# Widening float64 weights on VectorE and ScalarE alone, squaring in PSUM, and a new order of the first third

## The chip, the cores and the metric

The kernel runs on one core of one Trainium2 chip. Its metric is the device time of one execution in microseconds (us); 1429.37 us is the median of three executions before the change (1426.54 to 1430.47). The engines are named as the profile names them: PE is TensorE (PEld its weight loads), DVE is VectorE, ACT is ScalarE, POOL is GpSimd, and SP issues the DMAs. Each engine runs its own instructions in a fixed order and waits on semaphores for the others.

## What is computed

A linear attention with an exponential feature map, then a dense two-layer network with squared ReLU, then a mixture of four experts over all tokens:

```python
proj = x @ w_phi                                   # x is q or k: 4 batches, 8 heads, 576 tokens, 64 wide
proj = proj - max(abs(proj))                       # over the 128 features
phi  = concat(exp(proj), exp(-proj))
kv, z = phi(k).T @ v, sum(phi(k))
attn = (phi(q) @ kv) / (phi(q) @ z + 1e-6)         # 2304 tokens, 512 wide
h = relu(attn @ w_in)                              # 512 x 2048
x = (h * h) @ w_out                                # 2048 x 512
p = domain_probs / sum(domain_probs)
out = sum_e p[:, e] * (relu(x @ w1[e]) @ w2[e])    # 4 experts, 512 x 1024 x 512
```

`w_in` and `w_out` arrive as float64, and the kernel reads each number as two 32-bit words.

## The kernel before

Every product is made of three single-precision products: an operand is split into a rounded high part and the remainder, its low part, and low*high, high*low and high*high are summed in PSUM. A split is a copy (the method `copy`, line 78 on ACT, line 80 on DVE) and a subtraction (`sub`, line 83, on DVE or POOL).

The work has three stages. **The front** takes the first third of the time. In it 16 pairs of heads (`Pair`, four batches of four pairs) go through attention: transposes, a projection, `shift` (absolute maximum and subtraction, lines 231 and 239, on DVE), exponentials on ACT, and small matmuls. Beside them the first two batches go through the dense network: eight groups `fg` of two chunks of 128 hidden units, each chunk with two matrices (`Matrix`, one from `w_in`, one from `w_out`, so 32 in all, each 128 x 512), and for each group and batch a `Unit`: `hidden` (line 516), `relu`, `square`, `g_hi`, `g_lo` for two chunks, then four `out` (line 563) and `add` (line 571). Each of the 32 matrices is loaded, widened from float64 to single precision (lines 457 to 477), stored to DRAM for later use, and split (`hi` on ACT, `lo` on POOL). **The second stage** runs the dense network for the other two batches with a seven-product scheme (`PairUnit`), and **the third** the experts. Both are built from times in a plan (`plan_tail`) and follow on an unchanged code path.

All steps of the front, and the first of the second stage, stand in one table: `PLACES` gives each step of each object its place in one sequence (1788 places before), and the steps are issued in that sequence, so the table sets the order on every engine and on SP's DMA queue. The tile pools decide what waits for what: `ps_m` has three PSUM banks of 128 x 512 and holds the hidden products `ph`, the outputs `pm`, and in the first nine pairs the attention's small products; `ps_a` has three banks, `ps_p` one larger tile. A bank is given to the next product when its last reader is done.

In `widen`, four DVE instructions build the number's bits: `top` (line 457, a shift and a mask; line 460, the sign), `one` (line 464, the power of two), and `wf` (line 465, the low word times that power). POOL adds `top` to `wf` (line 470), ACT squares the high word (line 474) and DVE multiplies `wf` by a comparison with that square (line 477), which sets tiny numbers to zero. In `Unit`, ACT writes relu(ph) to an SBUF tile `r`, DVE overwrites `r` with max(ph, 0)*r (line 539), ACT copies it to `gh`, and POOL subtracts to get `gl`.

Of the kernel before, what the change touches and what calls it, by code (L numbers as in the profile page):

```python
# [8 lines left out]
F32 = mybir.dt.float32  # L9
# [12 lines left out]
def fused_kernel(  # L22
# [68 lines left out]
    make_identity(nc, ident)  # L91
    wd = const.tile([P, 2 * NF], F32, name="wd")
# [339 lines left out]
    class Matrix:  # L432
# [17 lines left out]
        def widen(self):  # L450
            self.f = pools["w"].tile([P] + self.shape, F32, tag=self.tag + "f", name="wf", bufs=WB[self.tag])
            self.dst = dst = self.f if len(self.shape) == 1 else self.f.rearrange("p k f -> p (k f)")
            low, high = self.raw[:, :, 0], self.raw[:, :, 1]
            self.top = top = cpool.tile([P, DM], U32, tag="top", name="top", bufs=1)
            self.one = one = cpool.tile([P, DM], U32, tag="one", name="one", bufs=2)
# [8 lines left out]
            nc.vector.tensor_scalar(out=one, in0=top, scalar1=0xFF800000, scalar2=None, op0=ALU.bitwise_and)  # L464
            nc.vector.scalar_tensor_tensor(  # L465
                out=dst, in0=low, scalar=2.0**-52, in1=f32(one), op0=ALU.mult, op1=ALU.mult
            )
# [4 lines left out]
        def widen_mask(self):  # L472

            nc.scalar.activation(out=f32(self.one), in_=f32(self.raw[:, :, 1]), func=AF.Square)

        def widen_flush(self):
            nc.vector.scalar_tensor_tensor(
                out=self.dst, in0=f32(self.one), scalar=(2.0**-15 * 1.125) ** 2, in1=self.dst,
                op0=ALU.is_ge, op1=ALU.mult,
            )  # L480
# [41 lines left out]
    class Unit:  # L522
# [14 lines left out]
        def square(self, i):  # L537
            r = self.r[i]
            nc.vector.scalar_tensor_tensor(
                out=r, in0=self.p.pop(i)[:, : self.n], scalar=0.0, in1=r, op0=ALU.max, op1=ALU.mult  # L540
            )
# [31 lines left out]
    def new_x2(b):  # L573
# [797 lines left out]
```

## Time and profile before

| | |
|---|---|
| median of three executions | 1429.37 us (1426.54 to 1430.47) |
| the profiled execution | 1428.52 us, of which the profile's span is 1426.7 us |
| granted TensorE clock, mean over the span | 0.989 |
| busy share of the span | PE 96%, DVE 69%, ACT 41%, POOL 54% |
| chain of work that ended last, by engine | PE 78%, DVE 13%, issue 3%, POOL 3%, ACT 2% |
| DMA | 97.41 MB, mean 68 GB/s |

Busy time is the union of an engine's instructions. PE's matmuls overlap, so a busy PE may still not be at its peak. An instruction of DVE or POOL that waits for access to memory counts as busy, so one that takes far longer than the shortest of its kind has waited. The chain is followed back from the last instruction, at each step to whatever released it.

### The profile page before, as it was taken

To read this page: it belongs to the slowest core of one execution; us is meant where nothing else is said; L and a number is where in the kernel's file an instruction comes from. 1 tells how busy PE (TensorE), PEld (TensorE's weight loads), DVE (VectorE), ACT (ScalarE), POOL (GpSimd) and SP (SyncE) were. 2 spreads that over 40 slices of the span, in tenths; PEclk is the share of its full clock that TensorE was granted. 3 is DMA by queue.
4 is the path that set the end of the run, shared out by engine and by line. 5 is a ranking of instruction groups with operands and counts; after the bars stand their busy time and mean duration, and the time that the engine had idled before them with its cause. 6 is when DMAs were issued, how large, how long until landed. Compare 5 with 4: busy or idle time off the path is not lost.

```text
span 1426.7 us, 18682 instructions
## 1 busy us (share of the span) xinstructions
PE 1371.4 (96%) x6906; PEld 1142.2 (80%) x6906; DVE 977.9 (69%) x1305; ACT 579.0 (41%) x1034; POOL 764.4 (54%) x541
## 2 busy tenths in 40 slices
PE   8899998999988999999999999999999999999998
PEld 6677787877765888887788888887788888888887
DVE  6888899999978465667655565558655555555554
ACT  5677786666644533424232223224231221322321
POOL 2666867676859675677544444444544343442430
PEclk9999999999999999999999999999999999999999
DMA  6343423444253111101111121111311020110102
GB/s 149 91 101 91 130 83 104 127 132 120 85 149 108 36 60 31 44 15 60 60 59 55 35 60 60 53 37 37 111 60 30 30 60 30 45 45 30 45 1 74
DMA packets 136938, 97.41 MB, mean 68 GB/s; under 512 B 70288, under 2 KB 113424, under 8 KB 136848
## 3 DMA queue, kind: packets, MB, share of 16 engines
q1 hardware_dynamic: 136848, 96.23, 23.0%
q8 instruction: 55, 0.90, 0.3%
q14 instruction: 35, 0.29, 0.1%
HBM read 80.32 MB, written 15.80 MB: 67 GB/s over the span
## 4 chain that ended last, share of the span: by engine, by line
PE 78%; DVE 13%; issue 3%; POOL 3%; ACT 2%; DVEq 0%; POOLq 0%; ACTq 0%
PE pa L1205 27%; PE pz L1130 7%; PE pv L1130 7%; PE px L1130 7%; PE pa L1183 7%; PE pa L1160 5%; PE py L1130 4%; PE pm L563 2%; PE ph L516 2%; DVE top L460 2%; PE pm L326 2%; DVE one L464 1%; PE pm L360 1%; DVE top L457 1%; DVE mx L231 1%
## 5 line engine op out<-in xcount | busy, mean ns | idle before, releaser
L83 POOL TENSOR_TENSOR w<-f,w 128x1024 fp32r<-128x1024 f32 (+1 forms) x80 | 184.9, 2329 | 277.7 <-ACT w L78 277.7
L1214 DVE SCALAR_TENSOR_TENSOR x<-pa,prob,x 128x512 f32<-128x512 f32 x270 | 201.8, 750 | 131.6 <-PE pa L1205 131.6
L1205 PE MATMUL pa<-w2l,gh 128*128 128x512 f32 x576 | 225.0, 391 | 3.5 <-DVE x L1214 2.8
L1205 PE MATMUL pa<-w2h,gl 128*128 128x512 f32 x576 | 224.8, 390 | 1.0 <-DVE gl L1108 1.0
L1205 PE MATMUL pa<-w2h,gh 128*128 128x512 f32 x576 | 224.8, 390 | 0.0
L1137 ACT ACTIVATE u<-px 128x512 f32<-128x512 f32 x40 | 23.9, 597 | 454.2 <-PE px L1130 452.8
L83 POOL TENSOR_TENSOR w2l<-f,w2h 128x1024 fp32r<-128x1024 f32 x40 | 96.0, 2400 | 141.3 <-ACT w2h L78 141.3
L1102 ACT ACTIVATE gh<-u 128x512 fp32r<-128x512 f32 x136 | 85.9, 631 | 166.3 <-DVE u L1140 151.5
L1205 PEld LDWEIGHTS pa<-w2l,gh 128*128 128x128 f32 x576 | 108.4, 188 | 26.3 <-DVE x L1214 3.2
L1205 PEld LDWEIGHTS pa<-w2h,gl 128*128 128x128 f32 x576 | 108.4, 188 | 24.4 <-DVE gl L1108 1.8
L1033 POOL TENSOR_TENSOR f<-f 128x256 f32<-128x256 f32 x160 | 125.2, 803 | 3.3
L1205 PEld LDWEIGHTS pa<-w2h,gh 128*128 128x128 f32 x576 | 108.5, 188 | 21.9
L83 POOL TENSOR_TENSOR q<-qf,q 128x128 fp32r<-128x128 f32 (+1 forms) x64 | 100.0, 1578 | 46.5 <-DVE q L80 42.6
L1130 PE MATMUL pv<-oh,w 128*128 128x512 f32 x320 | 98.6, 389 | 1.8 <-POOL w L83 1.8
L1130 PE MATMUL px<-oh,w 128*128 128x512 f32 x320 | 99.5, 392 | 0.0
L1130 PE MATMUL pz<-oh,w 128*128 128x512 f32 x320 | 98.7, 390 | 0.0
L1140 DVE TENSOR_TENSOR u<-pz,u 128x512 f32<-128x512 f32 x80 | 55.3, 691 | 51.3 <-PE pz L1130 50.3
L1108 DVE SCALAR_TENSOR_TENSOR gl<-u,gh 128x512 fp32r<-128x512 f32 x96 | 72.3, 762 | 24.9 <-ACT gh L1102 23.5
L78 ACT ACTIVATE w<-f 128x1024 fp32r<-128x1024 f32 (+1 forms) x80 | 77.0, 1009 | 10.8 <-POOL f L1033 10.8
L1140 DVE TENSOR_TENSOR u<-py,u 128x512 f32<-128x512 f32 x40 | 27.6, 690 | 76.0 <-PE py L1130 42.9
L470 POOL TENSOR_TENSOR wf<-wf,top 128x512 f32<-128x512 f32 x32 | 46.2, 1445 | 57.6 <-DVE wf L465 48.0
L1160 PEld LDWEIGHTS pa<-rest,w 128*128 128x128 f32 x576 | 73.7, 195 | 1.9
(150 smaller groups left out, 3332.3 us busy)
## 6 DMA issues: line engine op xcount, KB each, us to landing
f<-in_moe_w_dram SPq DMA_DIRECT2D x96, 256.0 KB
raw<-in_moe_w_in_dram SPq DMA_DIRECT2D x16, 512.0 KB
raw<-in_moe_w_out_dram SPq DMA_DIRECT2D x16, 512.0 KB
f<-in_moe_w_dram SPq DMA_DIRECT2D x64, 128.0 KB
rec<-one SPq DMA_DIRECT2D x32, 144.0 KB
qk<-in_q_dram SPq DMA_DIRECT2D x32, 128.0 KB
qk<-in_k_dram SPq DMA_DIRECT2D x32, 128.0 KB
va<-in_v_dram SPq DMA_DIRECT2D x32, 128.0 KB
```

The lines of the kernel that those rows point to most:

```text
L78: nc.scalar.activation(out=dst, in_=src, func=AF.Copy)
L83: eng.tensor_tensor(out=dst, in0=a, in1=b, op=ALU.subtract)
L470: nc.gpsimd.tensor_tensor(out=self.dst, in0=self.dst, in1=f32(self.top), op=ALU.add)
L1033: nc.gpsimd.tensor_tensor(out=s[:, i], in0=a, in1=b, op=op)
L1102: nc.scalar.activation(out=self.gh, in_=self.r, func=AF.Copy if self.square else AF.Relu)
L1108: nc.vector.scalar_tensor_tensor(out=self.gl, in0=self.src, scalar=0.0, in1=f32(self.gh), op0=ALU.max, op1=ALU.subtract)
L1130: nc.tensor.matmul(p, lhsT=a, rhs=m, start=start and i == 0, stop=i == len(ops) - 1, skip_group_check=not start)
L1140: nc.vector.tensor_tensor(out=self.u[out], in0=self.p[a], in1=self.u[b], op=ALU.add)
L1160: nc.tensor.matmul(q, lhsT=a[:, s, k], rhs=m[:, kk], start=kk + j == 0, stop=kk == KD - 1 and j == 2)
L1183: nc.tensor.matmul(self.p[:, :n], lhsT=a, rhs=m, start=i == 0, stop=i == len(ops) - 1)
L1205: nc.tensor.matmul(self.p, lhsT=a, rhs=m, start=i == 0, stop=i == len(ops) - 1)
L1214: nc.vector.scalar_tensor_tensor(out=o, in0=p, scalar=pe, in1=o, op0=ALU.mult, op1=ALU.add)
```

## The change

The 32 widenings no longer use POOL. Two DVE masks take the exponent bits (`power`) and the fraction bits (`wf`) out of the high word; ACT turns the exponent bits into those of a single-precision power of two, and the fraction bits into 1 + fraction; DVE adds the low word, puts the sign on the power, and multiplies. Per matrix that is five DVE instructions and two on ACT, where five on DVE, one on ACT and one on POOL stood. In `Unit` the square stays in the PSUM bank of the hidden product, ACT and DVE read it there, and the low half is a DVE subtraction in place of a POOL one. `PLACES` is a new table throughout, now of 1852 places. A one-column constant is added.

```diff
+    exponent = const.tile([P, 1], F32, name="exponent")
+    nc.gpsimd.memset(exponent, -8.0 * 0x38000000)
...
         def widen(self):
...
-            nc.vector.tensor_scalar(
-                out=top, in0=high, scalar1=3, scalar2=0x3FFFFFFF, op0=ALU.logical_shift_left, op1=ALU.bitwise_and
+            self.power = cpool.tile([P, DM], U32, tag="power", name="power", bufs=2)
+            for out_, mask in ((self.power, 0x7FF00000), (self.dst.bitcast(U32), 0x000FFFFF)):
+                nc.vector.tensor_scalar(out=out_, in0=high, scalar1=mask, scalar2=None, op0=ALU.bitwise_and)
+
+        def widen_power(self):
+            nc.scalar.activation(out=self.power, in_=self.power, func=AF.Relu, scale=8.0, bias=exponent)
+
+        def widen_one(self):
+            nc.scalar.activation(out=self.dst, in_=self.dst.bitcast(U32), func=AF.Copy, scale=2.0**-20, bias=1.0)
+
+        def widen_add(self):
+            nc.vector.scalar_tensor_tensor(
+                out=self.dst, in0=self.raw[:, :, 0], scalar=2.0**-52, in1=self.dst, op0=ALU.mult, op1=ALU.add
             )
+
+        def widen_sign(self):
             nc.vector.scalar_tensor_tensor(
-                out=top, in0=high, scalar=0xC0000000, in1=top, op0=ALU.bitwise_and, op1=ALU.bitwise_or
+                out=self.power, in0=self.raw[:, :, 1], scalar=0x80000000, in1=self.power,
+                op0=ALU.bitwise_and, op1=ALU.bitwise_or,
             )
...
-        def widen_add(self):
-            nc.gpsimd.tensor_tensor(out=self.dst, in0=self.dst, in1=f32(self.top), op=ALU.add)
...
+        def widen_mul(self):
+            nc.vector.tensor_tensor(out=self.dst, in0=self.dst, in1=f32(self.power), op=ALU.mult)
...
         def square(self, i):
...
+            p, r = self.p[i][:, : self.n], self.r.pop(i)
+            nc.vector.scalar_tensor_tensor(out=p, in0=p, scalar=0.0, in1=r, op0=ALU.max, op1=ALU.mult)
 
         def g_hi(self, i):
             gh = pools["g"].tile([P, 512], F32R, tag="gh", name="gh")
-            copy(nc.scalar, gh[:, : self.n], self.r[i])
+            copy(nc.scalar, gh[:, : self.n], self.p[i][:, : self.n])
 
         def g_lo(self, i):
             gl = pools["g"].tile([P, 512], F32R, tag="gl", name="gl")
-            sub(nc.gpsimd, gl[:, : self.n], self.r.pop(i), f32(self.g[i][0][:, : self.n]))
+            sub(nc.vector, gl[:, : self.n], self.p.pop(i)[:, : self.n], f32(self.g[i][0][:, : self.n]))
...
     PLACES = {
         ("", "load_wd"): (
-            1,
+            7,
         ),
...
```

DVE near the end of the front, where the last matrices are widened; `raw` holds the float64 words of one matrix, `wf` its widened form, `ph` a hidden product, `x2` an output sum. Before:

```order
L457 TENSOR_SCALAR top_4953<-raw_4862 128x512
L460 SCALAR_TENSOR_TENSOR top_4953<-raw_4862,top_4953 128x512
L464 TENSOR_SCALAR one_4954<-top_4953 128x512
L465 SCALAR_TENSOR_TENSOR wf_4952<-raw_4862,one_4954 128x512
L477 SCALAR_TENSOR_TENSOR wf_4889<-one_4891,wf_4889 128x512
L457 TENSOR_SCALAR top_4994<-raw_4983 128x512
L460 SCALAR_TENSOR_TENSOR top_4994<-raw_4983,top_4994 128x512
L464 TENSOR_SCALAR one_4995<-top_4994 128x512
L465 SCALAR_TENSOR_TENSOR wf_4993<-raw_4983,one_4995 128x512
L477 SCALAR_TENSOR_TENSOR wf_4952<-one_4954,wf_4952 128x512
```

After:

```order
L458 TENSOR_SCALAR power_4951<-raw_4922 128x512
L458 TENSOR_SCALAR wf_4950<-raw_4922 128x512
L481 TENSOR_TENSOR wf_4737<-wf_4737,power_4738 128x512
L541 SCALAR_TENSOR_TENSOR ph_4866<-ph_4866,r_4928 128x512
L571 TENSOR_TENSOR x2_1_104<-pm_4930,x2_1_104 128x512
L475 SCALAR_TENSOR_TENSOR power_4951<-raw_4922,power_4951 128x512
L470 SCALAR_TENSOR_TENSOR wf_4950<-raw_4922,wf_4950 128x512
L83 TENSOR_TENSOR gl_5001<-ph_4866,gh_4978 128x512
L481 TENSOR_TENSOR wf_4950<-wf_4950,power_4951 128x512
```

The block of four widening instructions in a row is broken into a pair, a pair and a single one, with reads of PSUM between them, and `gl` has come to DVE.

POOL in the second half of the front; `q` are the low parts of the query features (`2x512` is the large form), `wl` those of a weight matrix, `va` those of v. Before:

```order
L83 TENSOR_TENSOR gl_4337<-r_4145,gh_4326 128x512
L173 MEMSET va_4353 128x9x2
L83 TENSOR_TENSOR gl_4371<-r_4150,gh_4279 128x512
L83 TENSOR_TENSOR wl_4409<-wf_4300,wh_4389 128x512
L83 TENSOR_TENSOR q_4450<-qf_4238,q_4298 128x2x512
L83 TENSOR_TENSOR q_4450<-qf_4245,q_4298 128x2x64
L83 TENSOR_TENSOR q_4461<-qf_4245,q_4453 128x2x64
L470 TENSOR_TENSOR wf_4443<-wf_4443,top_4444 128x512
L470 TENSOR_TENSOR wf_4518<-wf_4518,top_4519 128x512
L83 TENSOR_TENSOR gl_4562<-r_4369,gh_4545 128x512
```

After:

```order
L83 TENSOR_TENSOR wl_4563<-wf_4363,wh_4487 128x512
L83 TENSOR_TENSOR q_4561<-qf_4434,q_4417 128x2x512
L83 TENSOR_TENSOR va_4724<-va_4403,va_4594 128x594
L83 TENSOR_TENSOR wl_4749<-wf_4429,wh_4648 128x512
L83 TENSOR_TENSOR q_4771<-qf_4632,q_4745 128x2x64
L83 TENSOR_TENSOR q_4773<-qf_4632,q_4747 128x2x64
L83 TENSOR_TENSOR wl_4796<-wf_4583,wh_4794 128x512
L83 TENSOR_TENSOR q_4771<-qf_4742,q_4745 128x2x512
```

The additions to `wf` and the `gl` subtractions are gone from POOL; `q`, `wl`, `va` and the division stay.

SP's queue at the start; `wd` is the feature projection's weight, `raw` a float64 matrix. Before:

```order
L145 DMA qk<-in_q_dram 128x4x64
L145 DMA qk<-in_k_dram 128x4x64
L98 DMA wd<-in_w_phi_dram 64x128
L99 DMA wd<-in_w_phi_dram 64x128
L444 DMA raw<-in_moe_w_in_dram 128x4x256
```

After:

```order
L446 DMA raw<-in_moe_w_out_dram 128x1024
L147 DMA qk<-in_q_dram 128x4x64
L147 DMA qk<-in_k_dram 128x4x64
L145 DMA qk<-in_q_dram 128x1x64
L145 DMA qk<-in_k_dram 128x1x64
L147 DMA va<-in_v_dram 128x4x64
L147 DMA qk<-in_q_dram 128x4x64
L147 DMA qk<-in_k_dram 128x4x64
L100 DMA wd<-in_w_phi_dram 64x128
L101 DMA wd<-in_w_phi_dram 64x128
```

A weight matrix is now loaded first, and `wd` has moved from the third and fourth place to the ninth and tenth. On PE the twenty warming transposes of the identity (line 191), which stood first, now stand behind five transposes of queries and keys.

## Rows read from the trace of the kernel before

**Rows 1.** Stretches: busy us of PE, PEld, DVE, ACT, POOL; clock; DMA.

```profile
200.00:300.00 100.00, 91.34 (x522) 76.12 (x521) 96.91 (x117) 67.53 (x139) 70.18 (x50) 0.98 0.40 112
...
490.00:600.00 110.00, 109.93 (x578) 94.51 (x577) 59.71 (x91) 40.98 (x64) 70.68 (x53) 1.00 0.14 44
600.00:1400.00 800.00, 793.24 (x3719) 664.26 (x3718) 477.98 (x651) 225.52 (x313) 365.85 (x254) 1.00 0.15 45
```

**Rows 2.** The same view, the front as one stretch.

```profile
0.00:440.00 440.00, 403.15 (x2316) 330.56 (x2317) 390.72 (x513) 286.82 (x619) 286.85 (x214) 0.98 0.41 114
```

**Rows 3.** Chain that ended last: the span by engine, 0 to 440 by line.

```profile
PE 78%; DVE 13%; issue 3%; POOL 3%; ACT 2%; DVEq 0%; POOLq 0%; ACTq 0%
...
by line: issue 9.6%; PE pm L563 7.7%; PE ph L516 7.3%; DVE top L460 7.1%; PE pm L326 6.7%; DVE one L464 3.9%; PE pm L360 3.9%; DVE top L457 3.7%; DVE mx L231 3.3%; PE pa L326 2.9%; DVE kf L83 2.8%; PE pp L223 2.7%; DVE x L571 2.4%; PE pp L2
```

**Rows 4.** DVE groups, 0 to 440: count, busy us, mean ns, idle before.

```profile
L460 DVE SCALAR_TENSOR_TENSOR top<-raw,top 128x512 uint32<-128x512 uint32 x32 | 47.9, 1497 | 1.1
...
L477 DVE SCALAR_TENSOR_TENSOR wf<-one,wf 128x512 f32<-128x512 f32 x32 | 38.0, 1190 | 1.1 <-POOL wf L470 0.8 <-ACT one L474 0.3
L571 DVE TENSOR_TENSOR x<-pm,x 128x512 f32<-128x512 f32 x49 | 32.7, 680 | 8.9 <-PE pm L563 8.6
L465 DVE SCALAR_TENSOR_TENSOR wf<-raw,one 128x512 f32<-128x512 uint32 x32 | 31.6, 988 | 1.7
L457 DVE TENSOR_SCALAR top<-raw 128x512 uint32<-128x512 uint32 x32 | 30.1, 941 | 1.8 <-POOL wf L470 1.8
L464 DVE TENSOR_SCALAR one<-top 128x512 uint32<-128x512 uint32 x32 | 25.4, 793 | 1.1
...
L83 DVE TENSOR_TENSOR tl<-pa,th 128x512 fp32r<-128x512 f32 x32 | 21.7, 679 | 5.6 <-ACT th L78 5.5
```

**Rows 5.** Those widening lines one by one: shortest, median, longest in ns.

```profile
L457 DVE TENSOR_SCALAR top<-raw x32: 409/788/2553, 12.4 to 426.9; 128x512 uint32<-128x512 uint32 x32
L460 DVE SCALAR_TENSOR_TENSOR top<-raw,top x32: 691/1655/2772, 12.9 to 427.8; 128x512 uint32<-128x512 uint32 x32
L464 DVE TENSOR_SCALAR one<-top x32: 426/428/2500, 13.6 to 429.5; 128x512 uint32<-128x512 uint32 x32
L465 DVE SCALAR_TENSOR_TENSOR wf<-raw,one x32: 691/693/1809, 14.1 to 430.1; 128x512 f32<-128x512 uint32 x32
L477 DVE SCALAR_TENSOR_TENSOR wf<-one,wf x32: 622/913/2582, 20.6 to 432.2; 128x512 f32<-128x512 f32 x32
```

**Rows 6.** POOL groups, 0 to 440, as in rows 4.

```profile
L83 POOL TENSOR_TENSOR q<-qf,q 128x1024 fp32r<-128x1024 f32 x32 | 79.1, 2473 | 32.5 <-DVE q L80 28.5 <-ACT q L78 3.2 <-DVE spread L385 0.7
L83 POOL TENSOR_TENSOR gl<-r,gh 128x512 fp32r<-128x512 f32 x32 | 47.7, 1492 | 14.5 <-ACT gh L78 14.5
L83 POOL TENSOR_TENSOR wl<-wf,wh 128x512 fp32r<-128x512 f32 x32 | 46.7, 1461 | 28.1 <-ACT wh L78 28.1
L470 POOL TENSOR_TENSOR wf<-wf,top 128x512 f32<-128x512 f32 x32 | 46.2, 1445 | 57.6 <-DVE wf L465 48.0 <-issue 7.2 <-PE pp L225 1.1
```

**Rows 7.** POOL's addition one by one, as in rows 5.

```profile
L470 POOL TENSOR_TENSOR wf<-wf,top x32: 1264/1295/2217, 14.9 to 430.8; 128x512 f32<-128x512 f32 x32
```

**Rows 8.** Chain from 405 to 468, by line.

```profile
by line: issue 23.7%; POOL f L1033 15.9%; POOL w L83 12.7%; POOL gl L83 7.0%; POOL wl L83 5.3%; POOL ol L83 5.2%; DVE wf L477 5.0%; POOL w2l L83 3.8%; PE pz L1130 2.9%; PE pa L1160 2.7%; DVE top L460 2.6%; POOL xs L402 2.3%; DVE one L464 2.
```

**Rows 9.** ACT groups, 0 to 440, as in rows 4.

```profile
L474 ACT ACTIVATE one<-raw 128x512 f32<-128x512 f32 x32 | 21.5, 672 | 30.1 <-DVE wf L465 27.8 <-issue 2.2
...
L78 ACT ACTIVATE gh<-r 128x512 fp32r<-128x512 f32 x32 | 19.6, 625 | 8.0 <-DVE r L539 8.0
L78 ACT ACTIVATE th<-pa 128x512 fp32r<-128x512 f32 x32 | 19.0, 599 | 12.4 <-PE pa L195 10.9 <-PE pp L225 1.2
```

**Rows 10.** The start in order of time: start us, duration us, instruction.

```profile
1.41 4.25 PE L191 MATMUL pa<-ident 128*128 128x128 f32 x20 [1.41 <-POOL ident masks.py:199]
2.82 0.60 SPq L99 DMA_DIRECT2D wd<-in_w_phi_dram  x1
5.10 0.29 DVE L80 CAST wd_h<-wd 128x256 fp32r<-128x256 f32 x1 [3.97 <-DMA wd<-in_w_phi_dram]
7.51 0.39 PE L223 MATMUL pp<-wd_h,tl 128*128 128x256 f32 x1 [1.41 <-DVE tl L83]
```

**Rows 11.** PE's waits, 130 to 490: waited for, us in total, times, longest.

```profile
PE pm L563 <- DVE x L571: 1.4, 1, 1.4
```

More of the change, by code (lines that the diff above doesn't have):

```diff
@@ L451, in widen @@
             self.f = pools["w"].tile([P] + self.shape, F32, tag=self.tag + "f", name="wf", bufs=WB[self.tag])
[L452 to L455, printed above, removed]
-            nc.vector.tensor_scalar(
-                out=top, in0=high, scalar1=3, scalar2=0x3FFFFFFF, op0=ALU.logical_shift_left, op1=ALU.bitwise_and
+            self.dst = self.f if len(self.shape) == 1 else self.f.rearrange("p k f -> p (k f)")
@@ new lines, in widen @@
+            high = self.raw[:, :, 1]
+            self.power = cpool.tile([P, DM], U32, tag="power", name="power", bufs=2)
[5 more added lines that the diff above has]
+            nc.scalar.activation(out=self.dst, in_=self.dst.bitcast(U32), func=AF.Copy, scale=2.0**-20, bias=1.0)
@@ L465, in widen @@
-            nc.vector.scalar_tensor_tensor(
-                out=dst, in0=low, scalar=2.0**-52, in1=f32(one), op0=ALU.mult, op1=ALU.mult
-            )
-        def widen_add(self):
-            nc.gpsimd.tensor_tensor(out=self.dst, in0=self.dst, in1=f32(self.top), op=ALU.add)
[L472 to L480, printed above, removed]
+                out=self.power, in0=self.raw[:, :, 1], scalar=0x80000000, in1=self.power,
@@ L734, in fused_kernel @@
-            1165, 1183, 1297, 1228, 1336, 1356, 1433, 1386, 1477, 1497, 1528, 1507, 1579,
+            81, 2, 216, 307, 599, 558, 428, 711, 709, 815, 778, 866, 886, 965, 947, 1041, 1000, 1125, 1093,
+            1189, 1183, 1318, 1255, 1367, 1278, 1441, 1390, 1519, 1491, 1583, 1560, 1626,
+        ),
+        ("Matrix", "widen_power"): (
+            87, 10, 281, 314, 626, 618, 429, 714, 729, 820, 779, 884, 892, 973, 956, 1049, 1013, 1138, 1097,
+            1201, 1185, 1331, 1277, 1371, 1282, 1470, 1408, 1535, 1528, 1605, 1562, 1641,
+        ),
@@ new lines, in fused_kernel @@
+            1205, 1194, 1335, 1275, 1394, 1322, 1487, 1410, 1534, 1531, 1602, 1578, 1643,
+        ),
+        ("Matrix", "widen_sign"): (
+            121, 11, 285, 315, 627, 632, 443, 765, 746, 845, 786, 905, 893, 977, 974, 1054, 1020, 1155, 1098,
+            1211, 1216, 1332, 1283, 1374, 1311, 1482, 1412, 1548, 1530, 1606, 1575, 1642,
+        ),
+        ("Matrix", "widen_mul"): (
+            149, 21, 286, 375, 660, 667, 509, 766, 761, 848, 812, 910, 939, 994, 1017, 1083, 1108, 1167, 1123,
+            1250, 1218, 1347, 1284, 1395, 1350, 1492, 1446, 1559, 1561, 1610, 1582, 1644,
@@ L817, in fused_kernel @@
         ),
         ("Rest", "make"): (
-            1657,
+            1718,
         ),
         ("Weights", "load"): (
-            1605, 1644, 1721, 1714,
+            1663, 1704, 1821, 1747,
         ),
         ("Weights", "load2"): (
-            1628, 1685, 1727,
+            1697, 1739, 1839,
         ),
         ("Weights", "sums"): (
-            1620, 1649, 1731,
+            1665, 1716, 1835,
         ),
         ("Weights", "hi"): (
-            1614, 1661, 1770,
+            1679, 1711, 1833,
@@ L832, in fused_kernel @@
         ),
         ("Weights", "lo"): (
-            1621, 1675, 1780,
+            1680, 1719, 1834,
         ),
         ("Weights", "hi_sums"): (
-            1629, 1651, 1742,
+            1681, 1733, 1836,
         ),
         ("Weights", "lo_sums"): (
-            1631, 1662, 1775,
+            1693, 1740, 1837,
         ),
         ("Weights", "hi2"): (
-            1640, 1689, 1765,
+            1730, 1745, 1844,
         ),
         ("Weights", "lo2"): (
-            1653, 1710, 1776,
+            1749, 1782, 1846,
@@ L921, in fused_kernel @@
         for m in ms[0] + ms[1]:
-            for name in ("load", "widen", "widen_add", "widen_mask", "widen_flush", "store", "hi", "lo"):
+            for name in ("load", "widen", "widen_power", "widen_one", "widen_add", "widen_sign", "widen_mul", "store", "hi", "lo"):
                 at(0, getattr(m, name))
```

163 lines of the change are left out of this document (75 added, 88 removed), and 91 rows, old and new, of the table PLACES.

## Prediction

> **What bounds the kernel now.** I read the stretches first, then the chain, then DVE's and POOL's groups in the stretch that the change touches, then the shortest and longest of the single lines. From 490 us on PE is busy 109.93 of 110 us and then 793.24 of 800 [rows 1]: there PE alone sets the time. The new table ends before that, and no instruction behind it changes, so I expect those 937 us to stay, and the change is worth what it does before 490.
>
> There the picture is another. Between 200 and 300 DVE is busy 96.91 of 100 us, PE 91.34 [rows 1]. Over the whole front, 0 to 440, DVE is busy 390.72 us, PE 403.15, ACT 286.82 and POOL 286.85 [rows 2]. PE's figure is a union of overlapping matmuls, so its queue holds less work than that; DVE's is nearly full but is not all work. The same widening instruction takes 691 ns at the shortest and 2772 at the longest (line 460); line 457 goes from 409 to 2553, line 464 from 426 to 2500 [rows 5]. What lies above the shortest is waiting. Per matrix the five shortest add up to 409 + 691 + 426 + 691 + 622 = 2839 ns, times 32 is 90.8 us; the busy times are 47.9 + 38.0 + 31.6 + 30.1 + 25.4 = 173.0 [rows 4]. So DVE waits 82.2 us inside these 160 instructions. An instruction that takes one of its operands from PSUM does not: `tl` averages 679 ns and the sum at line 571 averages 680 [rows 4]. POOL waits too: its addition takes 1264 ns at the shortest, 1445 on average and 2217 at the longest [rows 6, 7].
>
> The row fits one cause, that DVE and POOL shut each other out where both read two operands from SBUF. The Trainium skill says the same (SBUF — State Buffer, "Who interferes with whom"): the second port pair is an exclusive lock between the two engines, taken by a DVE instruction with two SBUF inputs or in a two-port mode, and not by one with at most one SBUF input. The trace agrees, with 2772 ns against the mean of 679 beside it. By that rule the move of `gl` from POOL to a PSUM operand on DVE takes no new lock.
>
> How much of it is on the path? In the chain from 0 to 440 lines 460, 464 and 457 hold 7.1 + 3.9 + 3.7 = 14.7%, or 64.7 us [rows 3], of their 103.4 us busy. Lines 465 and 477 are not among the entries down to 2.4% (10.6 us), so at most 10.6 each. That is up to 85.9 of 173.0, and I use one half for everything that becomes shorter or longer in the widening.
>
> **The change part by part.**
>
> *Widening on DVE.* Five instructions go and five come: two masks from the strided high word (nearest row line 457, 409 ns shortest), the addition with an integer and a float operand (line 465, 691), the sign (line 460, 691), the product (622 as line 477, also two SBUF operands). That is 2822 ns a matrix, 90.3 us in all: the bare work stays. If the masks ran like line 460, it would be 18 us more.
>
> *Their waits.* POOL loses the additions and the low halves of the squares, 46.2 + 47.7 = 93.9 of 286.85 us [rows 2, 6]. Two steps. A DVE instruction that meets POOL at work waits for the rest of what runs, so it counts busy time weighted by length: 79.1 x 2.473 + 47.7 x 1.492 + 46.7 x 1.461 + 46.2 x 1.445 = 402 for the four groups, and the remaining 67 us at an estimated 1.3 us make 87; of 489 the change takes 138, and 0.72 is left. And long waits need a POOL that has the next instruction ready each time DVE gives way; how often it has goes with its occupancy, which falls to 193 / 287 = 0.67. Product 0.48: the 82.2 us fall to 39.6, by 42.6, and half of it is 21 us of the path. The ends are 0 (the order puts the rest of POOL's work just where DVE widens) and 41 (no wait left). I take 21 because both of DVE's and POOL's rows show waits, so both have a backlog. The front's broken-up block of four points the same way: between widening instructions now stand reads of PSUM, in which POOL gets its turn for nothing.
>
> *The low halves of the squares.* 32 more DVE instructions like `tl`, 32 x 679 = 21.7 us. For instructions of this kind the chain has 10.6 (2.4% of 440) of 32.7 us of line 571 [rows 3, 4], 0.32, so +7.0; ends 0 and 21.7. The square itself now writes PSUM instead of SBUF, which no row of DVE shows; I take its time as unchanged, bounds minus 2 and plus 4. POOL's part disappears from the chain: 7.0% of 63 us, 4.4, near the front's end [rows 8]; ends 0 and 10.
>
> *ACT.* Two activations for one, 32 x 672 ns = 21.5 us more [rows 9]. ACT is busy 287 of 440 and holds 2% of 1426.7 us in the chain, 28.5 of its 579 us, one twentieth: +1.1. The cover is its idle third; without it 21.5. The copy to `gh` reads PSUM; the nearest such row is 599 ns against 625 [rows 9], so nothing.
>
> *The start.* The weight of the projection is in SBUF at 5.10 us and the first projection starts at 7.51 [rows 10]. It now stands six places later on SP's queue, at 0.60 us each, so it comes near 8.7; the 20 warming transposes (4.25 us) no longer fill the wait for the first load but stand behind it, from about 5.5 to 9.7. The first projection then starts near 10, 2.5 us later. The DVE widens its first matrix meanwhile, which it need not do later. I take +2, ends minus 1 and plus 4.
>
> *PSUM banks.* A hidden product keeps its bank for two more instructions, 625 + 679 ns [rows 4, 9], 32 times, 41.7 us of bank time over three banks. PE's wait for a bank is 1.4 us in all at line 563 [rows 11], so I take nothing; the upper end is a rival below.
>
> Sum: -21 + 7 - 4.4 + 1.1 + 2 = -15.3. Against the profiled execution of 1428.52 us (span 1426.7, 1.8 around it) that is 1413.2; the median is 0.85 above that execution, so **1414 us**. What is late next is PE itself: 403 of 440 us leave 37 to gain, and this takes two fifths of them.
>
> **The rivals.** A measurement of this kernel can tell a difference of about 0.3% (4.3 us) from none.
>
> *Only the running instruction is waited for.* If POOL seldom has a backlog, the waits fall only to 0.72, by 23 us, half on the path: -11.5 + 7 - 4.4 + 1.1 + 2 = -5.8, 1423.6 us, between 1419 and 1429. For it: POOL's additions have a median of 1295, close to the shortest [rows 7], so it was seldom held up. Against: line 460's median is 1655, over twice its shortest. That a lock costs what its holder has left, and no more, is also how the Trainium skill has it (the section named above).
>
> *The order keeps the two engines apart.* Waits nearly gone: -41 + 7 - 4.4 + 1.1 + 2 = -35.3, 1394 us. For it: POOL has 193 us of work for 400, and DVE has far more PSUM work than that to lay beside it. Against: order on a queue is not time, and both engines drift by whatever they wait for.
>
> *PSUM banks run short (slower).* While a square waits on ACT and DVE for its two halves, its bank is shut, and of three banks two are hidden products; the four outputs of the unit before then pass through one. If the added 41.7 us stood in PE's way in full, that were -15.3 + 41.7 = +26, 1456; it decides from 15.3 us, a third of it. At one half the time is +5.5, 1435. For it: `square` and `g_lo` stand behind other work on DVE, so the bank is shut for longer than the two durations. Against: the 1.4 us [rows 11].
>
> *The change does not do what it says.* The order lays POOL's long `q` (2473 ns) where DVE widens and the waits stay at 82: +7 - 4.4 + 1.1 + 2 = +5.7, 1435 us.
>
> **How the numbers follow.** Forecast 0.42 (its own range 1404 to 1422), the running instruction only 0.17, order keeps them apart 0.18, banks 0.15, waits stay 0.08. Faster by over 0.3% (below 1425.1): 0.40 of the forecast, 0.10 of the second, all of the third, 0.68. Same: 0.02 + 0.05 + 0.05 of the banks' mild end + 0.03 = 0.15. Slower 0.17. The range goes from 1393 (the third case, with the half of it below left out) to 1434 (which leaves out the worse halves of the last two).
>
> **What would show it.** In the profile after: from the steady stretch of PE on, the same 937 us; the five widening lines between 3.5 and 4.5 us a matrix together (5.4 before), DVE's share in 200 to 300 below 0.95, POOL's busy time in the front near 190 us; `gl` on DVE near 680 ns. The first projection near 10 us. Wrong would be: PE's waits for a bank at lines 516 and 563 above 10 us in total (banks); widening at 5.4 us a matrix and DVE still full (waits stay); the front ending more than 25 us early (order); or a difference behind 490 us, which none of the cases has.

## The result and the profile after

| | before | after |
|---|---|---|
| median of the executions on one chip | 1428.12 us (4) | 1415.17 us (1414.85 to 1418.12, 4) |
| ratio | | 0.9913 [0.9892, 0.9934] |
| profiled execution, span | 1428.52, 1426.7 us | 1418.12, 1416.3 us |

The change takes 12.4 us by the ratio (13 by the medians), against 15.3 forecast. The stretches of the changed kernel, as [rows 1, 2]:

```profile
0.00:440.00 440.00, 405.00 (x2344) 331.67 (x2345) 361.10 (x557) 304.74 (x653) 199.46 (x157) 0.99 0.42 117
200.00:300.00 100.00, 95.69 (x550) 80.48 (x550) 92.07 (x137) 74.68 (x158) 44.08 (x32) 1.00 0.43 117
490.00:600.00 110.00, 110.00 (x572) 94.65 (x572) 58.38 (x93) 38.60 (x58) 76.83 (x56) 1.00 0.15 47
600.00:1400.00 800.00, 793.27 (x3716) 664.68 (x3715) 474.61 (x651) 224.71 (x312) 354.04 (x247) 1.00 0.15 45
```

Between 200 and 300 DVE is down from 96.91 to 92.07 us and PE up from 91.34 to 95.69. In the front POOL falls from 286.85 to 199.46 us, DVE from 390.72 to 361.10 with 32 more instructions of work; ACT rises by 17.9. Behind 490 us PE is as full as before. How far the front has moved is seen at a place that both kernels reach with the same 4242 matmuls left to do, a run of matmuls of the second stage, before (line 1160) and after (line 1168, the same code):

```profile
520.85 2.32 PE L1160 MATMUL pa<-rest,w 128*128 128x256 f32 x18
```

```profile
509.61 1.59 PE L1168 MATMUL pa<-rest,w 128*128 128x256 f32 x12
```

It starts 11.24 us earlier; the spans differ by 10.4. So what the change gives lies ahead of this place. The two stretches up to it hold the same 2664 matmuls:

```profile
0.00:520.85 520.85, 477.28 (x2664) 391.36 (x2665) 442.38 (x570) 322.31 (x674) 348.48 (x252) 0.97 0.38 106
```

```profile
0.00:509.61 509.61, 471.78 (x2664) 386.65 (x2665) 398.68 (x602) 338.08 (x706) 244.48 (x189) 0.99 0.39 108
```

PE's idle time falls from 43.6 to 37.8 us, which is 5.7 of the 11.2; the other 5.5 are PE's busy time for the same matmuls, at a granted clock of 0.99 in place of 0.97. So about half of the gain goes with the clock: before, it is below 1 in seven of the 26 stretches of 20 us up to 520 us, after in three.

How the front got ahead, from the ends of PE's matmuls in the two traces (us; the share of the front's hidden and output matmuls that is done):

| | 1/8 | 4/8 | 6/8 | all |
|---|---|---|---|---|
| hidden, before | 164.0 | 283.1 | 370.6 | 434.4 |
| hidden, after | 170.3 | 282.6 | 363.7 | 420.3 |
| out, before | 189.1 | 315.3 | 402.9 | 448.9 |
| out, after | 199.1 | 321.3 | 394.3 | 441.1 |

It is 6 to 10 us behind at first, still 6 behind with the outputs at one half, and 8 to 14 us ahead at the end. DVE's groups after, as [rows 4]:

```profile
L475 DVE SCALAR_TENSOR_TENSOR power<-raw,power 128x512 uint32<-128x512 uint32 x32 | 28.8, 901 | 1.9 <-ACT power L462 1.8
L481 DVE TENSOR_TENSOR wf<-wf,power 128x512 f32<-128x512 f32 x32 | 26.3, 822 | 0.4
L470 DVE SCALAR_TENSOR_TENSOR wf<-raw,wf 128x512 f32<-128x512 uint32 x32 | 26.1, 818 | 4.1 <-ACT wf L466 4.1
...
L83 DVE TENSOR_TENSOR gl<-ph,gh 128x512 fp32r<-128x512 f32 x32 | 21.6, 682 | 7.2 <-ACT gh L78 7.0
L458 DVE TENSOR_SCALAR wf<-raw 128x512 uint32<-128x512 uint32 x32 | 19.2, 600 | 0.0
L458 DVE TENSOR_SCALAR power<-raw 128x512 uint32<-128x512 uint32 x32 | 18.7, 585 | 3.5 <-DMA raw<-in_moe_w_out_dram 3.4
```

The five widening lines are 119.1 us, 3.72 a matrix (5.41 before). Their shortest are 412, 412, 624, 673 and 675 ns, 2796 a matrix and 89.5 us in all, so 29.6 us of waits are left of 82.2.

### The profile page after: what moved, and what is told of

It reads as the page before. It is cut to its first block, busy times and chain, and to the rows that moved or that the text cites. A ratio compares the mean times of both kernels' runs of the same rounds, so it can differ in the third digit from the quotient of the medians.

```text
span 1416.3 us, 18594 instructions
## 1 busy us (share of the span) xinstructions
PE 1367.0 (97%) x6906; PEld 1138.8 (80%) x6906; DVE 928.3 (66%) x1337; ACT 594.5 (42%) x1066; POOL 660.6 (47%) x478
## 4 chain that ended last, share of the span: by engine, by line
PE 65%; DVE 3%; ACT 0%; issue 0%; DVEq 0%; ACTq 0%
PE pa L1213 27%; PE pz L1138 8%; PE px L1138 7%; PE pv L1138 7%; PE pa L1191 7%; PE pa L1168 5%; PE py L1138 4%; DVE ol L83 1%; DVE gl L1116 0%; DVE u L1148 0%; DVE rest L83 0%; DVE x L1222 0%; PE pm L563 0%; DVE x L571 0%; ACT gh L1110 0%
## 5 line engine op out<-in xcount | busy, mean ns | idle before, releaser
L83 POOL TENSOR_TENSOR q<-qf,q 128x1024 fp32r<-128x1024 f32 (+1 forms) x64 | 95.8, 1511 | 117.2 <-DVE q L80 64.2
L1041 POOL TENSOR_TENSOR f<-f 128x256 f32<-128x256 f32 x160 | 117.4, 756 | 8.3 <-DMA f<-w_i 5.0
L83 POOL TENSOR_TENSOR wl<-wf,wh 128x512 fp32r<-128x512 f32 x32 | 42.9, 1348 | 89.1 <-ACT wh L78 89.0
L1198 DVE TENSOR_TENSOR x<-pa,x 128x512 f32<-128x512 f32 (+1 forms) x84 | 49.5, 600 | 40.0 <-PE pa L1191 39.9
```

The costliest lines, as they stand in the source:

```text
L83: eng.tensor_tensor(out=dst, in0=a, in1=b, op=ALU.subtract)
L1041: nc.gpsimd.tensor_tensor(out=s[:, i], in0=a, in1=b, op=op)
L1198: nc.vector.tensor_tensor(out=x, in0=p, in1=x, op=ALU.add)
```

## What DVE waited for

The two traces tell more than these groups, if the widening instructions are taken one by one: what each lasts beyond the shortest of its line, put down to the POOL instruction that it lies beside the longest (all 160 of each trace).

| POOL instruction met | before: met, wait us | after: met, wait us |
|---|---|---|
| `q` 128x1024 | 21, 32.3 | 15, 11.6 |
| `gl` | 26, 20.4 | gone |
| `wl` | 17, 12.5 | 14, 5.9 |
| `xs` | 8, 7.4 | 5, 4.4 |
| `va`, small `q`, `xl` | 18, 7.6 | 13, 6.1 |
| the widening's addition | 4, 1.5 | gone |
| none | 66, 0.6 | 113, 1.7 |

Almost no instruction that meets no POOL work waits. `gl`, which the change takes off POOL, stood for 20.4 us; the addition for 1.5, since it runs when DVE has handed that matrix over. `q` costs POOL as much as before and costs DVE 21 us less:

```profile
L83 POOL TENSOR_TENSOR q<-qf,q 128x1024 fp32r<-128x1024 f32 x32 | 80.4, 2514 | 76.8 <-DVE q L80 53.2 <-ACT q L78 21.8 <-DMA raw<-in_moe_w_in_dram 1.8
L83 POOL TENSOR_TENSOR wl<-wf,wh 128x512 fp32r<-128x512 f32 x32 | 42.9, 1348 | 89.1 <-ACT wh L78 89.0
```

What it cost before, DVE and POOL in order of time:

```profile
259.16 1.29 POOL L83 TENSOR_TENSOR wl<-wf,wh 128x512 fp32r<-128x512 f32 x1
259.33 1.42 DVE L457 TENSOR_SCALAR top<-raw 128x512 uint32<-128x512 uint32 x1
260.41 2.60 POOL L83 TENSOR_TENSOR q<-qf,q 128x1024 fp32r<-128x1024 f32 x1
260.78 2.77 DVE L460 SCALAR_TENSOR_TENSOR top<-raw,top 128x512 uint32<-128x512 uint32 x1
```

Line 457 (409 ns alone) ends 0.29 us after `wl`. POOL has `q` ready and starts 0.37 us before DVE's next instruction does, and line 460 ends 0.55 us after `q`: it waited for the rest of one instruction, twice in a row. Seven of line 460's ten meetings with `q` are of this kind, with `q` 0.29 to 0.37 us ahead and 2.73 to 2.77 us each. The other lines show the same: of the 160 instructions before, 70 waited for over 0.1 us and outlasted the POOL instruction that they met, and they end 0.28 to 0.29 us after it (lines 457 and 464) or 0.55 to 0.56 (lines 460, 465 and 477). Line 457 reads only one operand from SBUF, and so does line 464; together they hold 17.0 + 11.8 = 28.8 of the 82.2 us. So the prediction's words "where both read two operands from SBUF" leave a third of the waits out. In the new order POOL stands idle for longer before what it is to split (`wl` 89.0 us, 28.1 before [rows 6]), and so, it seems, has less ready at such moments.

## The experiments

Ratios are to the kernel before on the same chip. The runs come from several chips, on which the kernel before took 1428.1 to 1429.5 us, so differences between runs by their medians are good to some 2 us. The waits are those of the five widening lines, POOL's busy time that of 0 to 440, a fixed stretch: the earlier the front ends, the more of the second stage's work on POOL lies in it.

| label | time us | ratio [95%] | waits us | POOL us |
|---|---|---|---|---|
| before | 1428 to 1429 | 1 | 82 | 287 |
| after | 1415.17 | 0.9913 [0.9892, 0.9934] | 30 | 199 |
| n_w0 | 1440.48 | 1.0083 [1.0070, 1.0096] | 30 | 226 |
| n_g0 | 1428.93 | 1.0001 [0.9992, 1.0010] | 48 | 235 |
| n_w0g0 | 1457.42 | 1.0190 [1.0175, 1.0205] | 54 | 262 |
| o_w1 | 1431.97 | 1.0021 [1.0011, 1.0032] | 61 | 235 |
| o_ms | 1426.93 | 0.9982 [0.9971, 0.9993] | 81 | 291 |
| n_dup | 1426.48 | 0.9977 [0.9964, 0.9990] | 50 | 232 |
| n_dupm | 1431.40 | 1.0014 [1.0005, 1.0024] | 45 | 245 |
| s2 | 1417.85 | 0.9919 [0.9902, 0.9935] | 30 | 198 |
| o_tiny | 1422.53 | 0.9956 [0.9942, 0.9969] | 73 | 253 |
| n_w0_tiny | 1437.91 | 1.0053 [1.0032, 1.0074] | 26 | 190 |
| n_nol | 1406.90 | 0.9844 [0.9830, 0.9859] | 23 | 168 |
| v_q | 1419.00 | 0.9929 [0.9914, 0.9944] | 21 | 159 |

### The change in parts: order, widening, squares

The new order with the old widening (n_w0), with the old `Unit`, its square in SBUF and its `gl` on POOL (n_g0), with both old (n_w0g0), and the old order with the new widening (o_w1). In n_w0 and n_w0g0 `one` has a bfloat16 copy for the comparison and `top` two buffers, for space.

```diff
 # n_w0, in the new order's step widen_add (the rest of the old widening is not shown)
-            nc.vector.scalar_tensor_tensor(
-                out=self.dst, in0=self.raw[:, :, 0], scalar=2.0**-52, in1=self.dst, op0=ALU.mult, op1=ALU.add
+            nc.gpsimd.tensor_tensor(out=self.dst, in0=self.dst, in1=f32(self.top), op=ALU.add)
 # n_g0, in g_lo (the old square and g_hi are not shown)
-            sub(nc.vector, gl[:, : self.n], self.p.pop(i)[:, : self.n], f32(self.g[i][0][:, : self.n]))
+            sub(nc.gpsimd, gl[:, : self.n], self.r.pop(i), f32(self.g[i][0][:, : self.n]))
```

> The new table with the old widening (POOL adds again; the comparison's square is kept as bfloat16 and the power of two in the widened tile, so that it fits). Theory W (the gain is DVE's fewer waits for POOL, about half of them on the path): POOL is busy some 43 us more in the front, the widening's waits rise from 30 to about 55 us, time 1415 + 12 = 1427 us. Rival O (the gain is the new table): 1415 to 1418 us whatever the waits do. Rival E (only the additions and low halves that stood in the chain at the front's end count): about +6, 1421 us.

> The new table and widening, but the square in SBUF and its low half on POOL as before. Theory W: POOL busy 47 us more, DVE 22 us less work, waits up by about 20 us: +10 - 7, 1418 us. Rival O: 1415 us. Rival E: low halves back in the chain at the end, 1419 us.

> The new table with both operations as before. Theory W: waits in the widening near 80 us again and the time near 1428 us. Rival O: the table carries the gain, 1415 to 1418 us. Rival E: 1426 us.

> The old table with the new widening alone (both activations at the place of the old one, the addition and the sign at the place of POOL's addition where that comes later, the product at the old product's place). Theory W: POOL has 46 us less, waits fall from 82 to about 55, time 1428 - 12 = 1416 to 1420 us. Rival O: 1428 us or more, since the table was not made for it. Rival E: 1424 us.

The theory of waits (W) and rival E miss all four. Rival O, the order alone, misses the three in the new order; only in the old order (o_w1) did it have the time right. From n_w0g0 the new widening takes 28.5 us (to n_g0), the new squares 16.9 (to n_w0), both together 42.3; in the old order the new widening costs 2.7. The new order with the old operations is 28 us slower than the old one. So neither the order alone nor the new widening alone holds the gain: the table fits the operations it was made for. The old order with the new squares, alone or with the new widening, was not run. And the waits do not set the time across orders: 61 us of them go with 1432, 30 with 1440. What the order does to them by itself is also seen here: with the old operations they fall from 82 to 54 us (n_w0g0), though the time rises. In n_g0 a place shows where a mismatch bites, PE's waits:

```profile
PE pm L564 <- POOL gl L83: 8.0, 2, 7.7
```

An output product stands 7.7 us for a `gl` that the table had placed for DVE. In n_w0 PE waits more for DVE's output sums:

```profile
PE pm L569 <- DVE x L577: 10.0, 6, 3.4
PE ph L523 <- DVE x L577: 5.9, 3, 2.8
```

These are 15.9 us, against 4.5 in the changed kernel.

### What in POOL's work costs DVE: reads or busy time

> The kernel before, with POOL's addition in the widening (L470, 46.2 us for 32) replaced by three fills of the same buffer: POOL is as busy and the order and the waits between engines are the same, but these 32 instructions no longer read two operands from SBUF. It leaves out that addition. Theory L (DVE's waits are those for the operands that POOL reads, and half of a wait is on the path): the waits of the five widening lines fall from 82 to about 55 us and the time to about 1415. Theory F (a table and its operations are one set; the time follows where in the table the front's last steps come out, not how long DVE waits): the waits fall the same, the time stays at 1422 to 1428.

> The changed kernel, with one more POOL instruction behind each of the 32 low halves of the weights: a difference of two SBUF operands into a buffer that nobody reads. Some 42 us more of POOL, all of it with two SBUF reads. L: the waits of the widening lines rise from 30 to 45 or 50 us, the time by 8 to 10, to about 1424. F: the waits rise as much, the time stays within 4 us of 1415.

> The same as the run with one more POOL instruction behind each low half, but with three fills in its place, which read nothing from SBUF: POOL is busy for longer at the same places, without operands to fetch. L: the waits stay near 30 us and the time within 3 us of 1415. F: within 4 us of 1415 too; the difference between this run and the one with operands is the price of the fetching alone.

```diff
 # o_ms, in the kernel before
-            nc.gpsimd.tensor_tensor(out=self.dst, in0=self.dst, in1=f32(self.top), op=ALU.add)
+            for _ in range(3):
+                nc.gpsimd.memset(self.dst, 0.0)
 # n_dup, in the changed kernel, behind each wl
             sub(eng, self.l, self.f, f32(self.h))
+            sub(eng, scratch, scratch, scratch)
 # n_dupm, there
+            for _ in range(3):
+                eng.memset(scratch, 0.0)
```

o_ms: the waits stay at 81 us and the time falls by 2.6; L had 55 us and 1415. The table above says why: the addition is hardly met (1.5 us), so to change it tells nothing of reads. My expectation had repeated the prediction's weighting.

n_dup and n_dupm do tell. DVE and POOL in n_dup, where the added instruction reads:

```profile
214.18 1.24 POOL L83 TENSOR_TENSOR scratch<-scratch 128x512 f32<-128x512 f32 x1
...
214.56 1.40 DVE L477 SCALAR_TENSOR_TENSOR power<-raw,power 128x512 uint32<-128x512 uint32 x1
215.38 2.83 POOL L83 TENSOR_TENSOR q<-qf,q 128x1024 fp32r<-128x1024 f32 x1
215.88 2.87 DVE L472 SCALAR_TENSOR_TENSOR wf<-raw,wf 128x512 f32<-128x512 uint32 x1
```

and in n_dupm, where it fills:

```profile
217.12 1.71 POOL L497 MEMSET scratch<- 128x512 f32 x3
...
217.52 0.62 DVE L477 SCALAR_TENSOR_TENSOR power<-raw,power 128x512 uint32<-128x512 uint32 x1
218.07 0.68 DVE L472 SCALAR_TENSOR_TENSOR wf<-raw,wf 128x512 f32<-128x512 uint32 x1
...
222.92 1.86 POOL L497 MEMSET scratch<- 128x512 f32 x3
...
223.57 0.74 DVE L460 TENSOR_SCALAR power<-raw 128x512 uint32<-128x512 uint32 x1
224.24 0.82 DVE L460 TENSOR_SCALAR wf<-raw 128x512 uint32<-128x512 uint32 x1
```

Beside a read, line 477 takes 1.40 us and line 472 2.87; beside the fills 0.62 and 0.68, their shortest. Of the seven two-operand instructions that lay longest beside a fill, none lost more than 0.06 us. The Trainium skill has this rule (SBUF — State Buffer, "Who interferes with whom"): two inputs from SBUF contend with a GpSimd instruction that reads SBUF, not with one that only writes it; these rows agree. The masks are another matter: all 23 beside fills were longer than alone, half of them 0.82 us for 0.41; each of them ends 0.28 us after the fill that it met, as line 457 does after `wl`. So a mask waits for the rest of a fill as well, though the fill reads nothing.

In time, though, the fills cost more than the reads: 16.2 us for 15 us of added waits, against 11.3 for 21. L had 8 to 10 for the reads and 0 to 3 for the fills, F at most 4 for both: F misses twice, L where it tells the two apart, in the time and in the waits (45 us with the fills, not near 30). What went with the time in these two runs is how much POOL had to do: the added instructions take 38.0 us in n_dup and 54.3 in n_dupm, 0.30 us of time for each us in both.

### The price of POOL's work in either order

> The kernel before, with POOL's addition in the widening cut to 8 of its 512 columns: the step stays where it is in every queue, but 46.2 us of POOL's work become some 5. It leaves out the rest of the addition. Theory P (time follows how long POOL is busy in the front, at the 0.30 us of time per us of POOL that the runs with 38 and 54 us more of it gave): 42 us less, 1416. Theory L (DVE's waits, half of them on the path): the waits fall from 82 to about 60 us, 1418. Theory F (a table and its operations are one set, and the old table has no use for a freer POOL, as the new widening in it showed): 1425 to 1430 whatever the waits do.

> The changed kernel, with the low half of each weight matrix on POOL (42.9 us for 32) cut to 8 columns, and the high half read by TensorE in its place: the matmuls and the order stay, POOL is freed of 40 us and no product waits for it. It leaves out the low halves. P: 0.30 of 40 us, 1403. L: the waits of the widening lines fall from 30 to about 15 us, 1408. F: 1412 to 1418, since POOL is no longer what the front waits for.

> The new order with the old widening, as in the run that took 1440, with POOL's addition cut to 8 columns: POOL is freed of its work, the step through its queue between two of DVE stays. It leaves out the rest of the addition. P: POOL has 40 us less, 12 us, 1428. If the length of the addition in the chain from mask to product is the cost: 1418 to 1422. If the step through POOL's queue is the cost, and not its length: 1435 to 1440.

> The changed kernel, with half of the sixteen-column-block low halves of q (16 of 32 of 2.51 us each) moved from POOL to DVE, where each reads two operands from SBUF and takes an estimated 1.3 us: POOL is freed of 40 us, DVE has 21 more. P: -12 for POOL and 0.32 of 21 for DVE, 1410. L: the new instructions wait too, and the sum is 1415 to 1418. F: DVE is the fuller engine and its queue is set to the column; each 1.3 us delays what stands behind, 1420 to 1430.

```diff
 # o_tiny (kernel before) and n_w0_tiny (n_w0)
-            nc.gpsimd.tensor_tensor(out=self.dst, in0=self.dst, in1=f32(self.top), op=ALU.add)
+            nc.gpsimd.tensor_tensor(
+                out=self.dst[:, :8], in0=self.dst[:, :8], in1=f32(self.top)[:, :8], op=ALU.add
+            )
 # n_nol, in lo
+            if self.wide:
+                f, h = (x if len(self.shape) == 1 else x[:, 0] for x in (self.f, f32(self.h)))
+                sub(eng, scratch, f[:, :8], h[:, :8])
+                self.l = self.h
+                return
 # v_q, in q_lo
-                    nc.gpsimd, self.q_tile(1, h)[:, :, o : o + m],
+                    nc.vector if n > 1 and self.c % 2 else nc.gpsimd, self.q_tile(1, h)[:, :, o : o + m],
```

The stretch 0 to 440 in n_nol, n_dup and n_dupm (POOL's is the fifth busy time):

```profile
0.00:440.00 440.00, 406.56 (x2357) 333.44 (x2358) 358.24 (x562) 308.90 (x659) 168.30 (x162) 1.00 0.42 117
```

```profile
0.00:440.00 440.00, 401.58 (x2316) 326.19 (x2317) 368.80 (x548) 301.85 (x650) 232.07 (x189) 0.99 0.41 115
```

```profile
0.00:440.00 440.00, 401.82 (x2319) 326.95 (x2319) 365.70 (x548) 302.12 (x650) 245.33 (x252) 0.99 0.41 114
```

Against the changed kernel (199.46 us of POOL, 1415.17): n_nol 31.2 us less of POOL and 8.3 us faster, 0.27 us per us; n_dup 32.6 more and 11.3 slower, 0.35; n_dupm 45.9 more and 16.2 slower, 0.35. In the old order, o_tiny has 33.5 us less and is 6.9 faster, 0.21. Counted by the edited instructions alone (38.0 and 54.3 us more, 35.7 less in n_nol and 35.6 in o_tiny) and by the ratios (9.1, 14.4, 9.9 and 6.3 us), it is 0.24, 0.27, 0.28 and 0.18. Four kernels in one order thus lie near a line, whose slope is known only to between 0.2 and 0.35. Of the forecasts, n_nol lies between P (1403) and L (1408, though with waits of 23 us and not 15) and well under F; o_tiny lies between L (1418, with 60 us, not 73) and F (1425), and P's 1416 is 6.5 off. POOL's time is thus worth something in either order, more in the new one. It is a rule of thumb for this front, though, not a mechanism: part of it comes by the clock. Up to the place with 4242 matmuls left, n_nol is 6.6 us ahead of the changed kernel, and 4.6 of these are PE's busy time (467.2 us, at a clock of 1.00).

One way from POOL to PE is seen in the kernel before. From 405 to 468 us its chain is 52% POOL [rows 8], from the front's `wl` and `gl` through POOL's first work for the second stage (`f`, `w`, `w2l`, `ol`) to PE, and PE waits there for POOL:

```profile
PE pz L1130 <- POOL ol L83: 1.9, 1, 1.9
PE pv L1130 <- POOL w L83: 1.8, 1, 1.8
PE pm L563 <- POOL wl L83: 1.5, 1, 1.5
```

In the changed kernel none of PE's waits there is for POOL, and the chain, which can be followed back to 437 us, does not name it:

```profile
by line: DVE ol L83 6.8%; PE pz L1138 4.8%; PE pm L563 4.7%; PE pa L1168 4.6%; PE pv L1138 4.3%; PE px L1138 4.3%; PE pa L1191 4.3%; DVE x L571 4.1%; issue 3.0%; DVE rest L83 2.8%; PE py L1138 2.6%; DVE u L1148 2.2%; DVEq L1148 0.0%
```

POOL starts on `f` 16 us earlier; before, then after:

```profile
439.26 3.46 POOL L1033 TENSOR_TENSOR f<-f 128x256 f32<-128x256 f32 x2
```

```profile
423.37 2.95 POOL L1041 TENSOR_TENSOR f<-f 128x256 f32<-128x256 f32 x4
```

What share of the gain this path is, no run tells.

n_w0_tiny shows where that rule ends (P had 1428). POOL has 36 us less than in n_w0 and the time falls by 2.6 only (4.3 by the ratios): 22.7 of the 25.3 us between n_w0 and the changed kernel stay, a time within the 1435 to 1440 that were forecast for a step through POOL's queue, whatever its length. POOL's waits there:

```profile
POOL wf L471 <- DVE wf L466: 40.5, 11, 6.4
...
POOL wf L471 <- issue: 19.1, 6, 4.5
```

The addition, 0.32 us long, holds POOL's queue for 40.5 us while DVE is not yet there, and for 19.1 in which the profile shows nothing that it waits for. But this is not peculiar to the new order: in the kernel before POOL stood at the same place for 57.6 us [rows 6], and there the same cut (o_tiny) gave 6.9 us back. So the forecast time came, and the cause that went with it is not shown. The places that the old widening takes in the new table, its bfloat16 copy and the other count of ACT's steps are left as rivals, and what the 22.7 us are stays open.

v_q takes POOL down to 159 us and DVE's waits to 21. The moved instructions on DVE:

```profile
L83 DVE TENSOR_TENSOR q<-qf,q 128x1024 fp32r<-128x1024 f32 x16 | 21.1, 1322 | 0.2
```

It is 3.8 us slower than the changed kernel by the medians and 2.3 by the ratios, whose intervals overlap; P and L had 1410 and 1415 to 1418, F 1420 to 1430, and it lies between the last two. POOL's 40.3 us less would be 8 to 14 by the line, so 21.1 us more on DVE cost some 10 to 18, an estimate of 0.5 to 0.85 per us from one run, where the prediction used 0.32. No run that keeps the whole computation beat the changed kernel.

### The start

> The changed kernel with its start put back as it was: the twenty warming transposes ahead of the first projection's load, that load second on SP's queue, and the first weight matrix widened only after the first two projections. The first projection then starts near 8 us and not at 13 to 15. If the 5 to 7 us that the start lost are on the path, the time is 1409 to 1411; if the front absorbs them before its last quarter, it stays at 1413 to 1417.

```diff
-            if self.b + self.c + t0 == 0:
+            if self.b + self.c == 0 and t0 == 4:
 # PLACES: load_wd 7 -> 1.5, its split 22 -> 12.5, the first matrix's load 0 -> 3.5, its widening 2..33 -> 27..44
```

In the changed kernel the load of the projection's weight and what follows:

```profile
6.99 0.55 SPq L100 DMA_DIRECT2D wd<-in_w_phi_dram  x1
...
9.84 0.29 DVE L80 CAST wd_h<-wd 128x256 fp32r<-128x256 f32 x1 [0.24 <-DMA wd<-in_w_phi_dram]
...
13.14 0.56 PE L225 MATMUL pa<-wd_h,tl 128*128 128x256 f32 x1
...
14.90 0.39 PE L225 MATMUL pp<-wd_h,tl 128*128 128x256 f32 x1 [0.86 <-DVE tl L83]
```

In s2:

```profile
2.81 0.60 SPq L101 DMA_DIRECT2D wd<-in_w_phi_dram  x1
...
11.36 1.09 PE L197 MATMUL pa<-ident,qk 128*128 128x128 f32 x4 [3.37 <-DMA qk<-in_k_dram]
...
12.10 0.56 PE L225 MATMUL pa<-wd_h,tl 128*128 128x256 f32 x1
...
13.86 0.58 PE L225 MATMUL pp<-wd_h,tl 128*128 128x256 f32 x1 [0.77 <-DVE tl L83]
```

The weight is there 4 us earlier and the projection only 1, since the table loads the next tokens late (3.37 us of PE's wait). PE stood idle instead of running the twenty transposes, and the granted clock falls. The stretches of s2:

```profile
8.00:14.00 6.00, 1.87 (x8) 1.60 (x8) 1.17 (x3) 0.88 (x2) 0.00 (x0) 0.70 0.49 112
14.00:20.00 6.00, 4.03 (x20) 3.67 (x20) 4.37 (x8) 2.12 (x5) 0.00 (x0) 0.73 0.94 231
20.00:32.00 12.00, 10.11 (x50) 7.48 (x50) 7.73 (x13) 6.42 (x15) 4.21 (x4) 0.72 0.26 64
```

The means of 0.70 to 0.73 say that part of each stretch ran at 1.2 GHz, the lower level; in the changed kernel it is 1.00, the upper, from 8 to 20 us, and the second matmul of the projection takes 0.28 us there and 0.41 here. So s2 is 3 us later than the changed kernel throughout the front, and its time cannot be told from it. The edit did not restore the start, and what the start costs stays open.

## Why the prediction came out near

**The waits.** Forecast 82.2 to 39.6 us, measured 29.6. The size is near, the working wrong in two places. The additions were given 67 of 489 parts of the waits, by busy time and length, and had 1.5 of 82.2: an operation weighs by when it runs, not only by how long POOL runs it. And one factor for POOL's occupancy stands for two things. 20.4 us left with `gl`, and 30 beside `q`, `wl` and `xs` (21, 7 and 3), which POOL runs as before. Part of that is the order, which alone takes the waits from 82 to 54 (n_w0g0); part is how much else POOL has to do, for in one order the waits beside `q` go from 11.6 to 19.1 us with n_dup's added work. To that extent the case "the order keeps the two engines apart" came true, in its cause and not in its price.

**One half of them on the path** (-21, with -4.4 for POOL's `gl`: 25.4 us for 87.4 us less of POOL, 0.29 per us). The runs within one order give 0.2 to 0.35 us per us of POOL, so this sum is of the right size; set against their change of the waits, their times give 0.55 (n_dup), 0.76 (o_tiny), 1.05 (n_dupm) and about 1.2 (n_nol), so no one share of the waits fits them, and a half is not what the gain is made of. POOL's `gl` was priced by its 7.0% of the chain from 405 to 468; the other 45% that POOL held there [rows 8] were given nothing of their own, and from 437 us on they are gone from the chain as well.

**The clock** (no term). The sum counts waits and work and takes the clock as given. Of the 11.2 us up to the second stage 5.5 are PE's busy time at a higher clock, as the two stretches of the result show. Within one kernel the time goes with the clock as well: eleven executions of the kernel before on one chip run from 1426.2 us at a mean clock of 0.995 to 1432.4 at 0.986. Why the changed kernel was granted more was not tried; that a sum without this term comes out within 3 us is in part luck.

**DVE's low halves** (+7.0): 682 ns each as forecast. The share of 0.32 on the path is likely too small, by v_q's 0.5 to 0.85; n_g0 could not price it, since it undoes the order's match as well.

**The other cases.** "Only the running instruction is waited for" had the mechanism of a single wait right, as the rows above show, and its time of 1423.6 wrong, since the meetings themselves became fewer (94 of 160 before, 47 after). "Banks run short" and "the waits stay" did not come.

**ACT** (+1.1): 17.9 us more busy time; its price alone was not tried. DVE now stands idle for it at lines 470 and 475, 5.9 us in all, by the groups above.

**The start** (+2): mis-sized. The first small projection starts at 13.14 and the first large one at 14.90 us, not near 10; at one eighth of the projections the front is 5.5 us late (36.0 against 30.5), and level again at one half (123.0 against 122.6).

**PSUM banks** (0): nearly right. PE's waits at line 563 after:

```profile
PE pm L563 <- DVE x L571: 4.5, 3, 3.4
PE pm L563 <- DVE gl L83: 4.2, 3, 2.0
```

The second may be for the operand or for a bank. The 1.4 us before [rows 11] were not all, since the square was then the last reader of a hidden product's bank:

```profile
PE pm L563 <- DVE r L539: 4.7, 2, 2.8
```

So 6.1 us became at most 8.7, below the 10 from which that rival was to show, and the 41.7 us of bank time are found nowhere.

**"No instruction behind it changes, so the change is worth what it does before 490"**: right. What the sum lacked beside the clock is what the parts showed: it priced each operation as if the order stood apart from it. The total was near with an order that had been fitted to these operations; the four other pairings of order and operations that were run came out 15 to 43 us above the forecast.

## What to carry to other kernels

Put down an engine's waits one instruction at a time to what the other engine runs at that moment, before you expect anything of taking work off it: the addition was a sixth of POOL's time and 2% of DVE's waits. An order set by hand and its operations are priced together; half of such a change can be slower than neither (n_w0 by 11 us, o_w1 by 3). Before you put a gain down to one engine's waits, compare PE's busy time and clock over the same matmuls in both traces: here half of the gain was there.

## What the runs showed of the hardware

- A two-operand DVE instruction beside POOL's fills takes its shortest time (0.62 to 0.69 us), beside POOL's reads up to 2.87. A mask with one strided operand beside fills takes 0.82 us for 0.41 in half of the cases and 0.58 to 1.11 in the others, and three fills that meet masks up to 2.02 us, with 517 ns the shortest of one.
- When DVE waits, it is for the rest of one POOL instruction: 70 of 70 end 0.28 to 0.29 us (one SBUF operand) or 0.55 to 0.56 us (two) after it. And POOL can have its next one running 0.37 us before DVE's next starts: two instructions in a row, 1.42 and 2.77 us for 0.41 and 0.69. The first of the two reads one operand from SBUF, so one is enough for such a wait.
- The same 2664 matmuls keep PE busy for 477.28 us at a mean granted clock of 0.97 and for 471.78 at 0.99.
